# Two moves on VectorE in a two-layer attention and MLP kernel: the low halves of normalized tiles, and the reciprocals of the softmax denominators

## The chip, the cores and the metric

The kernel runs on one core of one Trainium2 chip. The metric is the device time of one execution, in microseconds (us). The engines are named as in the profile: PE (TensorE), ACT (ScalarE), DVE (VectorE), POOL (GpSimd) and SP (SyncE, which here issues all DMAs from one queue, in order). PEld is the loading of weights into PE.

## The reference

The input is 2048 rows of 512 numbers. Two layers follow, each an attention (A) and an MLP (B), with the same weights in both layers:

```
x = x + A(layernorm(x));  x = x + B(layernorm(x))      # twice
A: q = x@wq in 32 heads of 16;  k = x@wk, v = x@wv, one head for all
   p = softmax(q k^T / 4) over 2048 keys;  A = concat(p v) @ wo
B: relu(x@w1) @ w2, with w1 512x1792 and w2 1792x512
```

## The kernel before

**Precision.** Dense products run in 16 bits with each operand split into a high half and a low half, xh = fp16(x) and xl = fp16(x - xh); a product is xh·wh + xl·wh + xh·wl. So every normalized tile needs both halves before it can be used. The program has a fast path, which is what is timed, and an exact path behind a flag that is computed at the end (`self.good` collects the guards for it); `self.exact` is False in the fast path.

**Units and steps.** A unit U is four heads for 512 queries in one layer: 64 units. A unit has 16 steps, one per 128 keys. A step makes scores (PE, tile fst), exponentials (ACT, tile fp) and the product with the values (PE, into facc). Some steps are "cut": DVE splits the exponentials into two 16-bit parts (`cut`, rows fp<-fp), and PE then multiplies these with 16-bit values (`cut_values`, rows facc<-fp,fvp) instead of 32-bit ones (`values`, rows facc<-fp,fva).

**After every second unit** the sums are normalized. `unit_sums` reads the attention output (foraw) and the denominators (flsum) back from DRAM. `unit_inverse` tests the denominators against two limits (the guards, into fgood), clamps them, takes reciprocals, stores these to DRAM (frd) and reads them back spread over partitions (frinv). `unit_norm` multiplies foraw by frinv and splits the result into the halves fot.

**After every eighth unit** `follow` starts a chain for 512 rows (four tiles of 128): output projection, residual, layernorm, MLP up and down, residual, and in layer 0 the layernorm and the keys and queries of layer 1. In a chain, `ln` handles tiles in pairs: statistics and normalization for both (fbst, fbmv, fxn), then `halved` for both, then `laid`, which issues one transposing DMA per tile from fxp into the operand of the next product (fxt, fxq or fxr). A chain does this at two places, behind the output projection (`added` in `chain`) and, in layer 0, behind the last MLP product (`finish`). The last chain, alone at the end, transposes on PE instead and doesn't call `halved`. The 16 tiles of the input are normalized ahead of all that by `begin` (4) and `rows` (12); the 12 go through `halved` too, all before the first chain (`self.asked` counts the chains asked for, and is 0 until then).

**Dense products between attention steps.** Dense work is a generator that yields after each small group of products. Products run in pairs (`batch`): two PSUM tiles fmisc take a first half each, a one-element copy (fseen) on DVE marks that half as done, then the second halves follow, then DVE empties them.

**The order of the work** is fixed when the program is built. A planner (`timed`, `choose`) looks ahead over scores, value products and dense work, and picks the next item for PE by an account (`_Account`) of when each engine, tile and DMA will be free, with costs from `duration`. The account prices a subtraction of 128x512 on POOL at 0.2 + 512/530 and on DVE at 0.15 + 512/960 microseconds. `cut_some`, `early_for` and `soon` read it too: cuts are taken only when the account has DVE free, `unit_inverse` and `unit_norm` are put off to a later step while their inputs are not there, and a generator pauses until its operands are there. Every engine then executes its instructions in the order in which they were issued.

Almost all instructions have line L193, a helper's, in the profile, so tiles tell them apart.

Of the kernel before, what the change touches and what calls it, by code (L numbers as in the profile page):

```python
# [9 lines left out]
F32 = mybir.dt.float32  # L10
# [5 lines left out]
ALU = mybir.AluOpType  # L16
AX = mybir.AxisListType.X
MAX, MUL, SUB, ADD = ALU.max, ALU.mult, ALU.subtract, ALU.add
# [3 lines left out]
D = 512  # L22
# [7 lines left out]
LMIN, LMAX = 64.0, 1e30  # L30
# [194 lines left out]
class _Net:  # L225
# [319 lines left out]
    def halved(self, xn):  # L545

        xp = self.wt("xp", [P, 2, D], F16, bufs=4)
        self.nc.vector.tensor_copy(xp[:, 0], xn)
        self.nc.gpsimd.tensor_sub(xp[:, 1], xn, xp[:, 0])
        return xp  # L550

    def laid(self, xp, s, to):
# [878 lines left out]
    def unit_inverse(self, U):  # L1431
        nc = self.nc
        o, l = self.ol[U]
        if not self.exact:
            for lim, op in ((LMIN, ALU.is_ge), (LMAX, ALU.is_le)):
                nc.vector.scalar_tensor_tensor(self.good, l[:, 0], lim, self.good, op0=op, op1=MUL)
            nc.vector.tensor_scalar(l[:, 0], l[:, 0], LMIN, LMAX, op0=MAX, op1=ALU.min)
        nc.vector.reciprocal(l[:, 1], l[:, 0])
        rd = self.dp.tile([8, D], F32, name=self.tag + "rd", bufs=2)
        nc.sync.dma_start(rd.rearrange("h (c x) -> h c x", x=32), l[:, 1])  # L1440
        r = self.wt("rinv", [P, D], bufs=1 if self.exact else 2)
        nc.sync.dma_start(r, rd[:, None, :].to_broadcast([8, DH, D]))
        self.ol[U] = (o, r)
# [490 lines left out]
```

## Time and profile before

| | |
|---|---|
| median of 3 runs | 2221.99 us (2221.96 to 2226.26) |
| the profiled execution's own time | 2222.0 us |
| its span, first to last instruction | 2220.2 us |
| granted TensorE clock | 0.997 |

A row of the profile names the line, the engine, the operation, the tiles as out<-in, the shapes and the count; then total busy us and mean ns of one, or in the timeline the start and the length in us, with the idle time before it and what ended it in brackets. Rows that say x2 or x24 merge neighbouring instructions.

### The profile page before, as it was taken

Reading aid. Unit: us, or ns where it says so; the run is one execution under the profiler, and the core shown is the slowest. Engines: PE = TensorE matmul, PEld = TensorE weight load, DVE = VectorE, ACT = ScalarE, POOL = GpSimd, SP = SyncE. Lnnn points to the kernel's source line nnn. Section 1 sums busy time; section 2 is a strip of 40 time slices with the busy share of each in tenths; the row PEclk is TensorE's granted clock in tenths of the full one; section 3 lists DMA queues with packets and bytes.
Section 4 is the critical chain, followed back from the end, with each engine's and each line's share of the span. In section 5 each row is a group of like instructions: output and inputs, shape, how many; then the busy total and the mean of one; then the engine's idle time right before and its main releaser. Section 6 shows DMA issues by size and latency. Waiting matters only on the chain.

```text
span 2220.2 us, 127161 instructions
## 1 busy us (share of the span) xinstructions
PE 2151.6 (97%) x59833; PEld 1305.7 (59%) x59833; DVE 1188.3 (54%) x1931; ACT 1981.0 (89%) x2112; POOL 278.8 (13%) x318
## 2 busy tenths in 40 slices
PE   7999999999999999999999999999999999999998
PEld 3444446656667755555556755566655666675543
DVE  6526545554665565545575676555635555544442
ACT  6999999999999999999988889988999999999910
POOL 6317720001200021000120021100000000100000
PEclk9999999999999999999999999999999999999999
DMA  6336633212322143221341154431124211321222
GB/s 155 84 116 186 196 96 100 69 40 60 83 95 69 46 120 64 74 68 40 89 134 64 39 143 143 145 86 66 40 74 119 68 47 63 84 63 56 75 78 73
DMA packets 182800, 195.07 MB, mean 88 GB/s; under 512 B 79560, under 2 KB 115960, under 8 KB 182008
## 3 DMA queue, kind: packets, MB, share of 16 engines
q1 hardware_dynamic: 182264, 186.83, 28.8%
q8 instruction: 469, 7.68, 1.4%
q14 instruction: 67, 0.55, 0.1%
HBM read 120.16 MB, written 51.87 MB: 77 GB/s over the span
## 4 chain that ended last, share of the span: by engine, by line
PE 80%; ACT 11%; DVE 3%; DMA 3%; issue 2%; POOL 1%; SPq 0%; ACTq 0%; POOLq 0%; DVEq 0%
PE facc L193 31%; PE fmisc L193 28%; PE fst L193 20%; ACT fp L193 11%; DMA frd<-flsum 1%; DVE fxt L193 1%; DMA frinv<-frd 1%; DVE fbst L193 1%; SPq L193 0%; POOL fxp L193 0%; DMA fqop<-fqd 0%; DVE faccs L193 0%; POOL fbmv L193 0%; DMA fxq<-fxp 0%; DMA fqd<-fqh 0%
## 5 line engine op out<-in xcount | busy, mean ns | idle before, releaser
L193 ACT ACTIVATE fp<-fst 128x1024 f32<-128x1024 f32 x2048 | 1948.9, 1030 | 127.7 <-PE fst L193 114.7
L193 PE MATMUL fst<-fqop,fkop 64*32 64x512 f16 x16384 | 965.3, 378 | 42.6 <-ACT fp L193 32.6
L193 PE MATMUL facc<-fp,fva 64*32 64x512 f32 x13632 | 955.5, 591 | 2.0 <-DVE faccs L193 1.2
L193 PEld LDWEIGHTS <-fkop 64*32 64x32 f16 x16384 | 392.7, 91 | 457.9 <-issue 355.2
L193 DVE TENSOR_TENSOR fp<-fp 128x1024 f16<-128x1024 f32 x344 | 463.0, 1398 | 267.4 <-ACT fp L193 267.3
L193 PEld LDWEIGHTS facc<-fp,fva 64*32 64x32 f32 x13632 | 311.1, 106 | 92.3 <-issue 27.1
L193 PEld LDWEIGHTS <-fw 64*32 64x32 f16 (+1 forms) x9576 | 221.4, 93 | 108.0 <-issue 34.5
L193 PE MATMUL fmisc<-fw,fhh 64*32 64x512 f16 x6272 | 280.2, 376 | 1.1 <-DVE fseen L193 0.5
L193 POOL TENSOR_SCALAR fbmv<-fbmv 128x1 f32<-128x1 f32 x64 | 18.7, 293 | 1553.3 <-DVE fbmv L193 1552.5
L193 PE MATMUL fmisc<-fxt,fw 64*32 64x512 f16 x5376 | 199.2, 376 | 1.2 <-issue 1.0
L193 PEld LDWEIGHTS <-fhh 64*32 64x32 f16 (+1 forms) x6384 | 144.1, 93 | 78.0 <-issue 32.8
L193 PE MATMUL fmisc<-fw,fhl 64*32 64x512 f16 x3136 | 181.7, 376 | 0.0
L193 PE MATMUL facc<-fp,fvp 64*32 64x512 f16 (+2 forms) x4128 | 166.5, 387 | 0.0
L193 DVE SCALAR_TENSOR_TENSOR fxt<-fmisc,fxt 128x512 f32<-128x512 f32 x140 | 91.5, 682 | 137.1 <-PE fmisc L193 136.9
L193 PE MATMUL fmisc<-fxq,fw 64*32 64x512 f16 x4032 | 157.4, 376 | 0.3 <-DVE fhl L193 0.2
L193 DVE COPY fseen<-fmisc 1x1 f32<-1x1 f32 x266 | 29.2, 141 | 223.7 <-PE fmisc L193 219.7
L193 DVE TENSOR_TENSOR faccs<-faccs,facc 128x512 f32<-128x512 f32 x116 | 79.6, 686 | 64.2 <-PE facc L193 54.7
L193 DVE TENSOR_SCALAR fhh<-fmisc 128x512 f16<-128x512 f32 x98 | 67.0, 684 | 82.4 <-PE fmisc L193 82.3
L193 PE MATMUL fmisc<-fwo,fot 64*32 64x512 f16 x2688 | 106.3, 376 | 3.9 <-DVE fqr L193 1.9
L193 PEld LDWEIGHTS <-fvp 64*32 64x32 f16 (+1 forms) x4128 | 88.2, 90 | 33.6 <-issue 8.3
L193 PEld LDWEIGHTS <-fhl 64*32 64x32 f16 (+1 forms) x3192 | 73.6, 93 | 28.8 <-issue 4.5
L193 PEld LDWEIGHTS <-fot 64*32 64x32 f16 (+1 forms) x2736 | 59.4, 93 | 41.7 <-issue 16.5
(157 smaller groups left out, 1222.2 us busy)
## 6 DMA issues: line engine op xcount, KB each, us to landing
fw<-fwd SPq DMA_DIRECT2D x224, 256.0 KB
fod<-faccs SPq DMA_DIRECT2D x62, 256.0 KB
fqop<-fqd SPq DMA_DIRECT2D x152, 98.0 KB
fxt<-in_A_x_dram SPq DMA_DIRECT2D x32, 256.0 KB
fqd<-fqh SPq DMA_DIRECT2D x64, 128.0 KB
foraw<-fod SPq DMA_DIRECT2D x31, 256.0 KB
frinv<-frd SPq DMA_DIRECT2D x31, 256.0 KB
faccs<-in_B_w_dram SPq DMA_DIRECT2D x28, 256.0 KB
```

Source lines behind the costliest of these rows:

```text
L193: r = fn(*a, **k)
```

## The change

In `halved`, the low half is subtracted on DVE instead of POOL once a chain has been asked for; the tiles before that stay on POOL. In `unit_inverse`, the clamped denominators go into the second half of the tile, the reciprocal is taken there in place, and the store to DRAM is issued; only then come the two guards, which read the unclamped denominators. The read-back stays behind the store.

```
         xp = self.wt("xp", [P, 2, D], F16, bufs=4)
         self.nc.vector.tensor_copy(xp[:, 0], xn)
-        self.nc.gpsimd.tensor_sub(xp[:, 1], xn, xp[:, 0])
+        (self.nc.vector if self.asked else self.nc.gpsimd).tensor_sub(xp[:, 1], xn, xp[:, 0])
         return xp
...
         o, l = self.ol[U]
         if not self.exact:
+            nc.vector.tensor_scalar(l[:, 1], l[:, 0], LMIN, LMAX, op0=MAX, op1=ALU.min)
+        nc.vector.reciprocal(l[:, 1], l[:, 0 if self.exact else 1])
+        rd = self.dp.tile([8, D], F32, name=self.tag + "rd", bufs=2)
+        nc.sync.dma_start(rd.rearrange("h (c x) -> h c x", x=32), l[:, 1])
+        if not self.exact:
             for lim, op in ((LMIN, ALU.is_ge), (LMAX, ALU.is_le)):
                 nc.vector.scalar_tensor_tensor(self.good, l[:, 0], lim, self.good, op0=op, op1=MUL)
-            nc.vector.tensor_scalar(l[:, 0], l[:, 0], LMIN, LMAX, op0=MAX, op1=ALU.min)
-        nc.vector.reciprocal(l[:, 1], l[:, 0])
-        rd = self.dp.tile([8, D], F32, name=self.tag + "rd", bufs=2)
-        nc.sync.dma_start(rd.rearrange("h (c x) -> h c x", x=32), l[:, 1])
         r = self.wt("rinv", [P, D], bufs=1 if self.exact else 2)
         nc.sync.dma_start(r, rd[:, None, :].to_broadcast([8, DH, D]))
```

## The prediction

> **What bounds the kernel.** I read the page's busy times first, then the sums by stretch, then the waits of TensorE.
>
> ```profile
> span 2220.2 us, 127161 instructions
> PE 2151.6 (97%) x59833; PEld 1305.7 (59%) x59833; DVE 1188.3 (54%) x1931; ACT 1981.0 (89%) x2112; POOL 278.8 (13%) x318
> ```
>
> The first moved subtraction stands at 317 us and the last at 1919 us, so the stretch that matters is 300 to 2090 us (columns: length, then busy us of PE, PEld, DVE, ACT, POOL):
>
> ```profile
> 300.00:2090.00 1790.00, 1759.00 (x52161) 1111.76 (x52153) 976.64 (x1502) 1673.20 (x1765) 116.49 (x155) 1.00 0.28 79
> ```
>
> PE is idle for 1790.00 - 1759.00 = 31.0 us of it, 1.7%, at a granted clock of 1.00. PE sets the time. DVE has 1790.00 - 976.64 = 813 us free. Any gain has to come out of those 31 us, or out of less work on PE. What PE says it waits for there (total us, times, longest):
>
> ```profile
> PE fst L193 <- ACT fp L193: 17.5, 42, 1.2
> ...
> PE fmisc L193 <- DVE fseen L193: 0.9, 3, 0.4
> PE facc L193 <- DVE faccs L193: 0.8, 1, 0.8
> ...
> PE fmisc L193 <- DMA fxq<-fxp: 0.6, 1, 0.6
> ```
>
> More than half of the idle time is PE waiting for an exponential: moments at which the dense work (projections, MLP) has run out, so that attention goes on at ACT's pace. The tiles of the change appear with 0.6 us. So the question is how much sooner or later the change brings dense work in those moments.
>
> **The change, part by part.** The moved operation and its neighbours, from the view of the tile fxp (min/median/max ns) and from the groups by form for the same stretch (total us, mean ns):
>
> ```profile
> L193 DVE CAST fxp<-fxn x44: 417/420/423, 316.9 to 1917.8; 128x512 f16<-128x512 f32 x44
> L193 POOL TENSOR_TENSOR fxp<-fxn,fxp x44: 1148/1270/3525, 317.4 to 1919.2; 128x512 f16<-128x512 f32 x44
> ...
> L193 DVE TENSOR_TENSOR fp<-fp 128x1024 f16<-128x1024 f32 x340 | 457.6, 1398 | 263.0 <-ACT fp L193 262.9
> ...
> L193 DVE TENSOR_TENSOR fot<-foraw,fot 128x512 f16<-128x512 f32 x27 | 18.7, 692 | 0.9
> ...
> L193 DVE SCALAR_TENSOR_TENSOR fgood<-flsum,fgood 128x32 f32<-128x32 f32 x54 | 15.0, 278 | 3.7 <-DMA flsum<-fod 2.8
> ```
>
> All 44 subtractions of this stretch move. On DVE one has the shape and types of fot<-foraw,fot, so I take 0.69 us: 44 x 0.69 = 30.4 us more on DVE, 44 x 1.27 = 55.9 us less on POOL. They come in pairs (two tiles, then two transposing DMAs), 22 pairs.
>
> *Term A, transposes sooner.* Two places show a pair on its way (DVE, POOL, SP, PE rows of the timeline):
>
> ```profile
> 548.42 0.75 DVE L193 CAST fxp<-fxn 128x512 f16<-128x512 f32 x2
> 549.09 2.27 DVE L193 SCALAR_TENSOR_TENSOR fgood<-flsum,fgood 128x32 f32<-128x32 f32 x2
> ...
> 551.61 0.35 DVE L193 RECIPROCAL flsum<-flsum 128x32 f32<-128x32 f32 x1
> 548.92 2.39 POOL L193 TENSOR_TENSOR fxp<-fxn,fxp 128x512 f16<-128x512 f32 x2 [1.00 <-DVE fxp L193]
> 550.21 2.65 SPq L193 DMA_TRANSPOSE fxq<-fxp  x2
> 552.96 0.53 SPq L193 DMA_DIRECT2D frd<-flsum  x1
> ```
>
> ```profile
> 1120.00 0.76 DVE L193 CAST fxp<-fxn 128x512 f16<-128x512 f32 x2
> 1120.67 0.68 DVE L193 TENSOR_TENSOR faccs<-faccs,facc 128x512 f32<-128x512 f32 x1
> 1121.27 3.01 DVE L193 TENSOR_TENSOR fp<-fp 128x1024 f16<-128x1024 f32 x2
> 1120.50 4.77 POOL L193 TENSOR_TENSOR fxp<-fxn,fxp 128x512 f16<-128x512 f32 x2 [0.99 <-DVE fxp L193]
> 1121.81 5.39 SPq L193 DMA_TRANSPOSE fxq<-fxp  x2
> 1128.52 0.41 PE L193 MATMUL fmisc<-fxq,fwkh 64*32 64x512 f16 x8 [0.59 <-DMA fxq<-fxp]
> ```
>
> Before, the pair's last low half ends 548.92 + 2.39 - 548.42 = 2.9 us after the first cast starts. On DVE it takes 0.42 + 0.69 + 0.42 + 0.69 = 2.2 us, so it is ready 0.7 us sooner. At 1120 the cuts of the exponentials (fp<-fp) on DVE and the subtraction on POOL held each other up: 4.77 us for a pair instead of 2.39. There the pair would be ready at 1122.2 instead of 1125.3, 3.0 us sooner. Each pair's transposes land this much earlier, but PE only gains where it idles until they land. I looked at the first product that reads each transposed block. In four places it comes within about 5 us of the second transpose's issue; at the other handovers 10 us or more lie between, filled with other dense work. The four, from the first subtraction to that product:
>
> ```profile
> 333.00:340.00 7.00, 5.91 (x129) 2.41 (x129) 0.33 (x2) 7.00 (x8) 2.39 (x2) 1.00 0.79 124
> 548.92:556.78 7.86, 6.53 (x153) 2.75 (x145) 2.94 (x5) 7.86 (x10) 2.39 (x2) 1.00 0.50 113
> 1120.50:1128.52 8.02, 5.43 (x122) 2.21 (x121) 6.91 (x7) 7.94 (x10) 4.77 (x2) 1.00 0.41 73
> 1445.02:1452.34 7.32, 6.42 (x139) 2.86 (x145) 3.79 (x4) 7.32 (x9) 2.85 (x2) 1.00 0.71 117
> ```
>
> PE is idle for 16%, 17%, 32% and 12% of them; the rest is attention that must be done anyway, so a wait shortened by d gives back d times that share. The shortenings are 0.7, 0.7, 3.0 and, with a POOL pair of 2.85 instead of 2.39, 1.2 us; times the shares: 0.1 + 0.1 + 1.0 + 0.1 = 1.3 us. Bounds: nothing, where the planner puts the products at the same place in PE's order; 5.6 us, where each shortening counts whole. I take -1.3.
>
> *Term B, what now stands behind the subtractions on DVE.* DVE works in order. A pair keeps it 2 x 0.69 = 1.38 us longer. Behind 17 of the 22 pairs other work follows without a long enough pause, usually the fseen copies that let the second half of a batch of products start, or the faccs additions that free the accumulators. First and last of them:
>
> ```profile
> 540.12 0.20 DVE L193 COPY fseen<-fmisc 1x1 f32<-1x1 f32 x2
> 1918.16 0.20 DVE L193 COPY fseen<-fmisc 1x1 f32<-1x1 f32 x2
> ```
>
> At three pairs the blocked DVE gives time back. The guards at 549.09 took 2.27 us for two, against a mean of 2 x 0.28, and two more rows show it again:
>
> ```profile
> 1429.02 2.29 DVE L193 SCALAR_TENSOR_TENSOR fgood<-flsum,fgood 128x32 f32<-128x32 f32 x2
> 1445.19 1.65 DVE L193 TENSOR_TENSOR foraw<-foraw,frinv 128x512 f32<-128x512 f32 x1
> ```
>
> That is about 1.7 + 1.7 + 1.0 = 4.4 us of DVE, and these three pairs delay nothing. The other 14 pairs delay what follows by up to 1.38 us: 19.3 us. PE's waits for fseen and faccs are 1.7 us in all so far, because scores and value products fill in. With that cover, the delay costs the idle share of the whole stretch: 19.3 x 1.7% = 0.3 us. If the cover is used up as in the four windows (17%) it costs 3.3 us, and 6.2 us at the 32% of the worst one. Below zero it can't go, since nothing behind a pair comes sooner. I take +0.3, the row for the stretch, since PE's waits there are nearest to it.
>
> *Term C, reciprocals ahead of the guards.* The clamp now writes l[:, 1], the reciprocal works in place, and the store and its read-back are issued with the same neighbours on SP; no queue entry is passed. Two guards of 0.28 us no longer stand before the store: 0.56 us. At 549 that is worth nothing by itself: the reciprocal ended at 551.96, but the store waited until 552.96 behind the two transposes on SP. What waits for the read-back is the multiply of the attention output:
>
> ```profile
> DVE foraw L193 <- DMA frinv<-frd: 8.5, 4, 3.3
> ```
>
> Four waits of 27 units. Each shortens by at most 0.56 us, 2.2 us in all; at the 17% idle share of the second window 0.4 us. I take -0.4; bounds 0 and -2.2. The guards come later by the clamp and the reciprocal, and nobody waits for them before the end.
>
> *Term D, cuts.* A step whose exponentials are cut into two 16-bit halves on DVE is cheaper on PE:
>
> ```profile
> 1124.98 1.05 PE L193 MATMUL facc<-fp,fva 64*32 64x512 f32 x16
> ...
> 1128.73 0.87 PE L193 MATMUL facc<-fp,fvp 64*32 64x512 bf16 x24
> ```
>
> 0.18 us for each of the 170 cut steps (340 halves). The planner cuts only when its own account has DVE free. DVE gets 30.4 - 4.4 = 26 us more of work; at 2 x 1.40 us per cut that is at most 9 cuts lost, 1.7 us. In proportion to DVE's 813 free us it is 3%, 5 cuts, 0.9 us; a lost chance is often followed by another one step later, so I take half, +0.4. More cuts than now is possible too, because the order is made anew: -1.7 as the other bound.
>
> Sum: -1.3 + 0.3 - 0.4 + 0.4 = -1.0 us. The profiled execution took 2222.0 us, 1.8 us outside the span, and the median of the runs is 2221.99, so the forecast is 2221.0.
>
> One edge of the move shows in this pair of rows, a POOL subtraction that reads SBUF beside a DVE operation with two SBUF inputs, which takes 1.54 us here:
>
> ```profile
> 563.29 1.59 POOL L193 TENSOR_TENSOR fkop<-fkv,fkop 16x512 f16<-16x512 f32 x1 [11.99 <-DVE fkop L193]
> 563.89 1.54 DVE L193 TENSOR_TENSOR foraw<-foraw,frinv 128x512 f32<-128x512 f32 x1
> ```
>
> [...]
>
> **The rivals.** *Handovers count whole (faster).* The shortenings of term A come whole, 5.6 us, and those of C too, 2.2 us, with B and D as taken: -7.1 us, 2214.9. For it: at 1120 PE did wait for the transpose itself. Against: that is one place of 22.
>
> *The subtractions hold up the second halves of batches (slower).* The place is the fseen copies behind a pair, and it decides where a pair's batch has its second half still to come and no other dense work is open. Then the 14 pairs cost 6.2 us, the cuts 1.7, less 1.3 and 0.4: +6.2 us, 2228.2. For it: at 540 and 1918 the copies stand directly behind the casts, so DVE is already late there. Against: PE's wait for fseen is 0.9 us.
>
> *The order is made anew.* The planner accounts the subtraction on DVE and the earlier store, so from the first unit on its choices can differ everywhere, with no cause in one place. If a tenth of the 31 us of idle time and a tenth of the 170 cuts (17 x 0.18 = 3.1 us) go one way, that is 6.2 us: 2215 or 2228.
>
> *It does nothing.* The store waits behind the transposes as at 552.96, and the tiles were covered anyway: 2222.0. That lies inside the forecast's case.
>
> **How the numbers follow.** Runs of this kernel tell a change from none at about 0.2%, 4.4 us: 2217.6 to 2226.4. Forecast (with the case of nothing) 0.42, own range 2218 to 2225. Handovers whole 0.23; subtractions in the way 0.16; a new order that is better 0.11, worse 0.08. So faster 0.34, within 0.42, slower 0.24. The time is that of the likeliest, 2221.0. The range takes in both rivals' times and half as much again of the new order, 2211 to 2230.
>
> **What would show it.** Right: 12 subtractions on POOL and 44 on DVE at 0.69 us; no guard near 1.2 us beside one; a pair's casts and subtractions in 2.2 us; PE's waits for fseen and faccs under 3 us and its idle time in the stretch 27 to 34 us; 165 to 175 cuts. Wrong: PE idle 6 us more with fseen or faccs as releaser (slower rival), idle 5 us less in the windows before the transposed tiles (faster rival), or a number of cuts or idle places that moved where no pair and no unit is near (new order).

## The result and the profile after

The changed kernel takes 2238.8 us in the median (2233.96 to 2243.14) against 2221.99 us before (2219.23 to 2226.26): a ratio of 1.0075, with a 95% interval of 1.006 to 1.009. It is slower by 17 us. The forecast was 2221.0 us, a change too small to be told from none.

Single executions of one kernel scatter by some 5 us to either side. So below, a verdict on a kernel is always its ratio to the kernel before, timed on the same chip; a profile, which is one execution, is used for places and mechanisms. The profiled execution of the changed kernel took 2239.67 us. Its busy times:

```profile
span 2237.9 us, 127153 instructions
PE 2161.5 (97%) x59849; PEld 1250.8 (56%) x59849; DVE 1211.0 (54%) x1979; ACT 1981.5 (89%) x2112; POOL 223.9 (10%) x274
```

The span is 17.7 us longer. PE is busy 9.9 us longer (2161.5 against 2151.6) with 16 products more (59849 against 59833), and idle 7.8 us longer (76.4 against 68.6). Both have to be explained. POOL gave up 54.9 us and DVE took on 22.7 us, about as worked out.

The tiles of the two edits (min/median/max ns), then the cuts, from the page's groups:

```profile
L193 DVE CAST fxp<-fxn x44: 417/420/458, 315.7 to 1933.2; 128x512 f16<-128x512 f32 x44
L193 DVE TENSOR_TENSOR fxp<-fxn,fxp x44: 691/692/694, 316.1 to 1933.6; 128x512 f16<-128x512 f32 x44
L193 DVE SCALAR_TENSOR_TENSOR fgood<-flsum,fgood x54: 125/160/194, 365.4 to 2084.0; 128x32 f32<-128x32 f32 x54
```

```profile
L193 DVE TENSOR_TENSOR fp<-fp 128x1024 f16<-128x1024 f32 x348 | 467.4, 1394 | 236.2 <-ACT fp L193 235.9
```

The 44 subtractions take 0.692 us each, the guards at most 0.194 us, and 348 halves are 174 cut steps, 344 of them (172 steps) between 300 and 2105 us. The same guards before:

```profile
L193 DVE SCALAR_TENSOR_TENSOR fgood<-flsum,fgood x54: 164/192/1159, 361.8 to 2063.0; 128x32 f32<-128x32 f32 x54
```

What PE waits for between 300 and 2105 us (total us, times, longest):

```profile
PE fst L193 <- ACT fp L193: 19.1, 45, 1.0
PE facc L193 <- DVE faccs L193: 5.7, 4, 2.4
PE fmisc L193 <- issue: 5.4, 9, 1.0
PE fst L193 <- issue: 4.8, 5, 1.6
PE fmisc L193 <- DVE fseen L193: 0.8, 3, 0.3
PE facc L193 <- DVE fseen L193: 0.6, 1, 0.6
```

Before, faccs stood there with 0.8 us, once, and fseen with 0.9. The wait for a transposed block (fxq, 0.6 us) is gone; that is the gain the change was read for. In its place come 4.9 us more of waiting for accumulators, some more for exponentials (17.5 before), and 3.2 us more of "issue", idle time for which the profile shows no releaser.

A long wait and what stands ahead of it, from the timeline of the changed kernel:

```profile
315.66 0.42 DVE L193 CAST fxp<-fxn 128x512 f16<-128x512 f32 x1
316.11 0.69 DVE L193 TENSOR_TENSOR fxp<-fxn,fxp 128x512 f16<-128x512 f32 x1
316.72 0.42 DVE L193 CAST fxp<-fxn 128x512 f16<-128x512 f32 x1
317.17 0.69 DVE L193 TENSOR_TENSOR fxp<-fxn,fxp 128x512 f16<-128x512 f32 x1
317.78 0.68 DVE L193 TENSOR_TENSOR faccs<-faccs,facc 128x512 f32<-128x512 f32 x1
...
318.52 0.66 PE L193 MATMUL facc<-fp,fva 64*32 64x512 f32 x7 [2.38 <-DVE faccs L193]
```

The pair takes 317.17 + 0.69 - 315.66 = 2.2 us, as predicted. But an accumulator's last addition stands behind it, and PE's next product for that accumulator waits for it: 2.38 us. In the kernel before, the corresponding additions stand ahead of the layernorm and of the pair's casts, so nothing of the pair is in their way:

```profile
309.80 0.69 DVE L193 COPY faccs<-facc 128x512 f32<-128x512 f32 x1 [4.90 <-PE facc L193]
310.60 0.69 DVE L193 TENSOR_TENSOR faccs<-faccs,facc 128x512 f32<-128x512 f32 x1
...
312.17 0.69 DVE L193 SCALAR_TENSOR_TENSOR fxt<-fmisc,fxt 128x512 f32<-128x512 f32 x1 [0.89 <-PE fmisc L193]
...
316.95 0.76 DVE L193 CAST fxp<-fxn 128x512 f16<-128x512 f32 x2
```

So two things differ at this one place: the order, and what the order puts behind the subtractions. That is what the experiments take apart.

### The profile page after: what moved, and what is told of

The parts are those of the page before. It is cut to its first block, busy times and chain, and to the rows that moved or that the text cites. A ratio compares the mean times of both kernels' runs of the same rounds, so it can differ in the third digit from the quotient of the medians.

```text
span 2237.9 us, 127153 instructions
## 1 busy us (share of the span) xinstructions
PE 2161.5 (97%) x59849; PEld 1250.8 (56%) x59849; DVE 1211.0 (54%) x1979; ACT 1981.5 (89%) x2112; POOL 223.9 (10%) x274
## 4 chain that ended last, share of the span: by engine, by line
PE 81%; ACT 13%; DVE 3%; issue 2%; POOL 0%; DMA 0%; SPq 0%; ACTq 0%; DVEq 0%; POOLq 0%
PE facc L193 32%; PE fmisc L193 29%; PE fst L193 20%; ACT fp L193 13%; DVE fbst L193 0%; DVE fxt L193 0%; DVE fkop L193 0%; DVE faccs L193 0%; DVE fxp L193 0%; DVE fp L193 0%; POOL fbmv L193 0%; DVE fkv L193 0%; DVE fxn L193 0%; DMA fqop<-fqd 0%; SPq L193 0%
## 5 line engine op out<-in xcount | busy, mean ns | idle before, releaser
L193 PEld LDWEIGHTS <-fkop 64*32 64x32 f16 x16384 | 387.1, 91 | 483.1 <-issue 369.0
L193 PEld LDWEIGHTS facc<-fp,fva 64*32 64x32 f32 x13600 | 303.9, 106 | 106.5 <-issue 23.6
L193 PEld LDWEIGHTS <-fw 64*32 64x32 f16 (+1 forms) x9576 | 206.3, 93 | 123.0 <-issue 34.4
L193 PEld LDWEIGHTS <-fhh 64*32 64x32 f16 (+1 forms) x6384 | 135.4, 93 | 88.8 <-issue 32.6
L193 PE MATMUL facc<-fp,fvp 64*32 64x512 bf16 (+2 forms) x4176 | 166.0, 386 | 0.2 <-issue 0.2
L193 PEld LDWEIGHTS <-fvp 64*32 64x32 f16 (+1 forms) x4176 | 82.3, 90 | 40.2 <-issue 8.9
```

The costliest lines, as they stand in the source:

```text
L193: r = fn(*a, **k)
```

## The experiments

Two theories. *The hold-up*: 44 x 0.69 us more on DVE delay what stands behind them, wherever that is. *The order*: the planner's account reads the subtraction as DVE work and the store as earlier, and from there on builds another order of all engines, which happens to be slower. The kernels below differ only in which engine executes an operation, when, and in what the account is told, which can be set apart: `account` in the diffs charges an operation that is executed elsewhere.

All comparisons in one table; each interval is 95%.

| kernel | order of the work | low halves on | guards | ratio to before |
|---|---|---|---|---|
| second edit alone | new | POOL | behind | 1.0024 [1.0011, 1.0036] |
| first edit alone | new | DVE | ahead | 1.0042 [1.0029, 1.0056] |
| both, order of before | before | DVE | behind | 1.0066 [1.0049, 1.0083] |
| neither, order of after | after | POOL | ahead | 1.0057 [1.0039, 1.0075] |
| tiles 0, 1 alone | before | DVE for half | ahead | 1.0022 [1.0010, 1.0034] |
| tiles 2, 3 alone | before | DVE for half | ahead | 1.0049 [1.0034, 1.0065] |
| before, redrawn 0.21 | new | POOL | ahead | 1.0011 [0.9998, 1.0024] |
| before, redrawn 0.19 | new | POOL | ahead | 1.0020 [1.0004, 1.0035] |
| after, timed again | after | DVE | behind | 1.0090 [1.0073, 1.0106] |
| neither, both entries, 0.21 | new | POOL | ahead | 1.0076 [1.0062, 1.0091] |
| neither, both entries, 0.19 | new | POOL | ahead | 1.0064 [1.0049, 1.0080] |
| after, redrawn 0.21 | as two above | DVE | behind | 1.0109 [1.0092, 1.0126] |
| neither, entry of the first edit | as first edit alone | POOL | ahead | 1.0028 [1.0018, 1.0039] |
| the same, 0.21 | new | POOL | ahead | 1.0033 [1.0020, 1.0046] |
| second edit alone, 0.21 | new | POOL | behind | 1.0035 [1.0021, 1.0049] |
| second edit alone, 0.19 | new | POOL | behind | 1.0031 [1.0016, 1.0045] |
| second edit, order of before | before | POOL | behind | 0.9994 [0.9982, 1.0005] |
| guards ahead, order of the second edit | as second edit alone | POOL | ahead | 1.0036 [1.0022, 1.0050] |

"Redrawn" kernels have another price in the account, for every operation on POOL, so that the planner builds another order without any operation moving to another engine. A row that names an order of another row has the same instructions on PE and ACT, and the same DMAs on SP, in the same order as that row.

### Each edit alone

First the kernel with only the lines of `unit_inverse` changed, then the one with only the line of `halved`:

```
         if not self.exact:
+            nc.vector.tensor_scalar(l[:, 1], l[:, 0], LMIN, LMAX, op0=MAX, op1=ALU.min)
+        nc.vector.reciprocal(l[:, 1], l[:, 0 if self.exact else 1])
...
```

```
-        self.nc.gpsimd.tensor_sub(xp[:, 1], xn, xp[:, 0])
+        (self.nc.vector if self.asked else self.nc.gpsimd).tensor_sub(xp[:, 1], xn, xp[:, 0])
```

> Only the second edit: the reciprocals and their store ahead of the guards, the low halves stay on POOL. Theory 1 (the subtractions on DVE hold up what stands behind them, above all the faccs additions that free the accumulators): no subtraction has moved, so 2219 to 2225 us, and PE's wait for faccs stays near 0.8 us. Theory 2 (the planner's new order is worse by itself): the earlier store changes the account too, so any time between 2215 and 2240 us is possible.

> Only the first edit: the low halves on DVE, the guards ahead of the reciprocals as before. Theory 1: the whole loss is here, 2234 to 2244 us, with some 5 us of PE waiting for faccs. Theory 2: again a new order, any time between 2215 and 2245 us.

Measured 1.0024 and 1.0042. Neither edit is free, and the two sum to 0.66%, near the whole. The hold-up alone expected nothing in the first and the whole loss in the second, 2234 to 2244 us; the medians are 2222.6 and 2227.2 us, beside 2218.1 us for the kernel before on that chip. So the hold-up is not all of it; how much each way costs this doesn't yet say.

### The edits with the order held fixed

The changed operations are executed, but the account is charged as before, so that PE, ACT and SP get the work of the kernel before in the same order:

```
-        self.nc.gpsimd.tensor_sub(xp[:, 1], xn, xp[:, 0])
+        if self.asked:
+            self.tc.nc.vector.tensor_sub(xp[:, 1], xn, xp[:, 0])          # real
+            self.account("POOL", "tensor_sub", xp[:, 1], [xn, xp[:, 0]])  # charged
... # unit_inverse likewise: order of after executed, order of before charged
```

> Both edits are executed, but the planner's account is charged as if they were not: PE, ACT and SP get exactly the order of the kernel before. Theory 1 (direct hold-up on DVE): still slower than before, 2232 to 2245 us, with PE waiting for faccs or fseen at pairs. Theory 2 (the order is what costs): 2218 to 2224 us.

And the reverse: POOL subtracts and the guards stand ahead, as before, but the account is charged as after, which gives exactly the order of after:

```
-        self.nc.gpsimd.tensor_sub(xp[:, 1], xn, xp[:, 0])
+        if self.asked:
+            self.tc.nc.gpsimd.tensor_sub(xp[:, 1], xn, xp[:, 0])          # real
+            self.account("DVE", "tensor_sub", xp[:, 1], [xn, xp[:, 0]])   # charged
... # unit_inverse likewise: order of before executed, order of after charged
```

> The reverse: neither edit is executed (low halves on POOL, guards first), but the account is charged as if they were, so that PE, ACT and SP get exactly the order of the changed kernel. Theory 1: 2218 to 2226 us, since DVE no longer holds anything up. Theory 2: 2233 to 2244 us, like the changed kernel.

Measured 1.0066 and 1.0057. Each of the two alone makes more than half of the loss, and they don't add up: in the order of before the operations cost 0.66%, in the order of after only what is left to the changed kernel, 0.75 - 0.57 = 0.18% by its first comparison.

In the first of the two nothing but the moved operations differs from the kernel before. What PE waits for there, 300 to 2120 us:

```profile
PE fst L193 <- ACT fp L193: 16.8, 41, 1.2
PE fmisc L193 <- DVE fseen L193: 10.1, 10, 1.7
PE fmisc L193 <- issue: 3.1, 4, 0.9
PE facc L193 <- DVE fseen L193: 2.5, 3, 1.5
```

PE waits 10.1 + 2.5 = 12.6 us for fseen, 0.9 before. Not all of that is new idle time: between 300 and 2090 us PE is idle for 1790.00 - 1750.97 = 39.0 us against 31.0, since other waits grew shorter. One of the ten, from its timeline:

```profile
538.81 0.42 DVE L193 CAST fxp<-fxn 128x512 f16<-128x512 f32 x1
...
539.26 0.69 DVE L550 TENSOR_TENSOR fxp<-fxn,fxp 128x512 f16<-128x512 f32 x1
...
539.87 0.42 DVE L193 CAST fxp<-fxn 128x512 f16<-128x512 f32 x1
...
540.33 0.69 DVE L550 TENSOR_TENSOR fxp<-fxn,fxp 128x512 f16<-128x512 f32 x1
540.94 0.20 DVE L193 COPY fseen<-fmisc 1x1 f32<-1x1 f32 x2
541.19 0.63 PE L193 MATMUL fmisc<-fw,fhh 64*32 64x512 f16 x16 [0.83 <-DVE fseen L193]
```

Before, the same copies stood at 540.12 (the prediction quotes the row) directly behind the casts, and PE's products show no wait:

```profile
539.45 0.76 DVE L193 CAST fxp<-fxn 128x512 f16<-128x512 f32 x2
...
540.69 0.74 PE L193 MATMUL fmisc<-fw,fhh 64*32 64x512 f16 x16
```

One step of scores and values covered the copies, but not 1.38 us more.

In the second, the order of after with POOL's subtractions, the place at 316 us shows the order's own part. Its timeline:

```profile
314.50 0.76 DVE L193 CAST fxp<-fxn 128x512 f16<-128x512 f32 x2
315.17 0.68 DVE L193 TENSOR_TENSOR faccs<-faccs,facc 128x512 f32<-128x512 f32 x1
...
315.90 0.66 PE L193 MATMUL facc<-fp,fva 64*32 64x512 f32 x7 [0.93 <-DVE faccs L193]
```

PE waits 0.93 us for the late addition even without the subtractions; with both on DVE, 2 x 0.69 us later, it waits 2.38 us. At this place the order makes the collision, and the subtractions lengthen it. It is one place of 0.93 us. In the profiled execution of this kernel, the fastest of its six (2223.2 us), PE is idle for 1805.00 - 1772.85 = 32.2 us between 300 and 2105 us, 31.0 before; so this profile doesn't show where the rest of the order's 0.57% goes.

### Which pairs hold up

In the order of before, only the first pair at each of a chain's places on DVE (tiles 0 and 1), or only the second (2 and 3):

```
+    def halved(self, xn, r=None):
...
+        if r is not None and r < 2:     # or: r > 1
+            self.tc.nc.vector.tensor_sub(xp[:, 1], xn, xp[:, 0])
+            self.account("POOL", "tensor_sub", xp[:, 1], [xn, xp[:, 0]])
```

> In the order of the kernel before (the account is not told), only the first pair of each handover (tiles 0 and 1) has its low halves on DVE: 22 subtractions; guards as before. Theory 1a (what is lost is the fseen copies that stand behind first pairs and let a batch's second half start): nearly all of the direct loss, 8 to 13 us more than before, with 8 to 12 us of PE waiting for fseen. Theory 1b (any pair on DVE costs alike): half of it, 5 to 8 us.

> The same for the second pair (tiles 2 and 3), behind which the handover to the next product comes. Theory 1a: no loss or a small gain from the earlier transposes, between 5 us less and 2 us more than before. Theory 1b: 5 to 8 us more.

Measured 1.0022 and 1.0049: both cost, the second pairs more, so the expected division between them was wrong. PE's waits for fseen, first in the kernel with the first pairs, then in the one with the second:

```profile
PE fmisc L193 <- DVE fseen L193: 5.7, 7, 1.6
```

```profile
PE fmisc L193 <- DVE fseen L193: 5.4, 6, 1.7
...
PE facc L193 <- DVE fseen L193: 2.6, 3, 1.6
```

Together 13.7 us, about the 12.6 us of both at once, and 0.22 + 0.49 = 0.71% is about the 0.66%. So the hold-up looks like a sum over places. That the second pairs cost more than twice the first with 8.0 against 5.7 us of these waits is not explained.

### Is any new order slower?

The kernel before with the account's fixed price of an operation on POOL at 0.21 or 0.19 us in place of 0.2:

```
-            return 0.2 + n / 530
+            return 0.21 + n / 530      # or 0.19
```

> The kernel before with nothing changed but one price in the planner's account: an operation on POOL costs 0.21 in place of 0.20 us plus its length. The work and the engines are the same and the order on PE is another one. Theory 2a (a redrawn order is by itself slower than the one the kernel had): 4 to 12 us more than before. Theory 2b (the order of the changed kernel is worse because the account knows of the busier DVE): within 4 us of before.

> The same with a price of 0.19 us. Theory 2a: 4 to 12 us more than before. Theory 2b: within 4 us of before.

Measured 1.0011 and 1.0020. A new order alone, without any moved work, costs 0.1 to 0.2% in these two draws, the first of which can't be told from nothing: the order of before seems to be a good draw. So part of every new order's cost may be only that. The next four ask whether orders from a busier account are worse than that: the changed kernel again, the engines of before with both edits' entries in the account under both prices, and the changed kernel under the first:

```
+            self.tc.nc.gpsimd.tensor_sub(xp[:, 1], xn, xp[:, 0])          # as in neither, order of after
+            self.account("DVE", "tensor_sub", xp[:, 1], [xn, xp[:, 0]])
...
-            return 0.2 + n / 530
+            return 0.21 + n / 530      # or 0.19
```

> The changed kernel once more, on the chip of the runs it stands beside here. By the first comparison 0.6 to 0.9% slower than before. If direct hold-up and order simply added up it would be 1.2%.

> Engines of before, with an account charged as if both edits were made (as in the run with the order of after), and the account's price of a POOL operation at 0.21 in place of 0.20 us, so that the order is redrawn. Theory 3a (an account that knows of the busier DVE makes worse orders in general): 0.35 to 0.7% slower than before. Theory 3b (the order of the changed kernel was an unlucky draw): 0 to 0.25% slower, like the two redraws of the kernel before.

> The same with 0.19 us. Theory 3a: 0.35 to 0.7% slower than before. Theory 3b: 0 to 0.25%.

> The changed kernel, both edits executed and accounted, with the price at 0.21: exactly the order on PE, ACT and SP of the first redraw with a busy account, so the difference of the two is the direct effect of the edits in an order that knows of them. Direct hold-up: 0.1 to 0.4% slower than that redraw, with PE waits for faccs and fseen. No hold-up left once the planner knows: equal within 0.1%.

Measured 1.0090, 1.0076, 1.0064 and 1.0109. The three orders built with both entries but run with the engines of before (with the 1.0057 above) lie at 0.57 to 0.76%, above both plain redraws. On top of that come the executed edits. In the redrawn order, on one chip, they cost 1.09 - 0.76 = 0.33%, in the order of after 0.90 - 0.57 = 0.33% or, with the first comparison, 0.18%; each is uncertain by about 0.23% (the two half-widths, 0.16 each, combined as squares). That is 4 to 7 us of 2220.

### Which entry makes the order

Only the entry of the first edit, engines as before; then the same with the price 0.21 on POOL:

```
+            self.tc.nc.gpsimd.tensor_sub(xp[:, 1], xn, xp[:, 0])
+            self.sim.run("DVE", ..., duration("DVE", "tensor_sub", ...))
```

> Engines of before; the account is charged for the low halves on DVE alone (not for the second edit): on PE, ACT and SP exactly the order of the run with only the first edit. Theory 4a (it takes both entries in the account to make the bad orders): 0 to 0.25% slower than before. Theory 4b (the entry for the low halves is enough): 0.4 to 0.75%. Theory 4c (the entry for the earlier store is what does it): 0 to 0.25%.

> The same, redrawn with a POOL price of 0.21 us. Theory 4a: 0 to 0.25% slower than before. 4b: 0.4 to 0.75%. 4c: 0 to 0.25%.

The second edit alone under two more prices, 0.21 and then 0.19:

> Only the second edit, executed and accounted, redrawn with a POOL price of 0.21 us. Theory 4a and 4b: 0.1 to 0.3% slower than before, like the first draw of it. Theory 4c: 0.4 to 0.75%.

> The same with 0.19 us. Theory 4a and 4b: 0.1 to 0.3% slower than before. Theory 4c: 0.4 to 0.75%.

Measured 1.0028 and 1.0033 for the first entry, 1.0035 and 1.0031 for the second edit (1.0024 above). Each makes an order that is about 0.3% slower. That lies between the expectations, of which one kind was up to 0.25 or 0.3% and the other from 0.4% on. The first edit, executed in the order of its own entry, costs 0.42 - 0.28 = 0.14% on top, uncertain by 0.17%.

Last, the second edit taken apart like both were: executed in the order of before (shown), and its order with the guards executed ahead as before:

```
         if not self.exact:
+            for _ in range(2):
+                self.account("DVE", "scalar_tensor_tensor", self.good, [l[:, 0], self.good])
+            self.account("DVE", "tensor_scalar", l[:, 0], [l[:, 0]])
+            self.account("DVE", "reciprocal", l[:, 1], [l[:, 0]])
+            real.tensor_scalar(l[:, 1], l[:, 0], LMIN, LMAX, op0=MAX, op1=ALU.min)
+        real.reciprocal(l[:, 1], l[:, 0 if self.exact else 1])
... # the store, then the guards on real, not charged again
```

> Only the second edit, executed but not accounted: reciprocals ahead of the guards in exactly the order of the kernel before on PE, ACT and SP. Theory 5a (the second edit costs only through the order that its entry makes): 2214 to 2219 us, within 0.1% of before or a little faster, since only the store leaves sooner. Theory 5b (something of the edit itself costs): 4 to 9 us more than before.

> The reverse: guards first as in the kernel before, the account charged for the second edit, so that PE, ACT and SP have the order of the run with only the second edit. Theory 5a: 4 to 9 us more than before. Theory 5b: within 0.15% of before.

Measured 0.9994 [0.9982, 1.0005] and 1.0036. Executing the second edit costs nothing that can be measured; its 0.3% is the order. The first of the two has the lowest ratio of all, and it can't be told from the kernel before.

## Why the prediction was wrong, step by step

The loss of the changed kernel, 0.75% and 0.90% in its two comparisons, is made of three parts that the runs set apart, each to within some 0.2%: about 0.3% for the order from the first entry, about 0.3% for the order from the second (0.57% for both together), and 0.1 to 0.3% (3 to 7 us) for what the subtractions hold up within an order that was made for them. These are times as measured, so each holds its share of slower clock, which the last section bounds.

- **Term B failed: its price.** The prediction had the mechanism and the amount of delay, 19.3 us over 14 pairs, and priced it by the idle share of the whole stretch, 1.7%: +0.3 us. In the order of before, where nothing else differs, PE's waits for fseen grew by 12.6 - 0.9 = 11.7 us, 61% of the 19.3, and the time by 0.66% (14.6 us). That is also far above the 6.2 us that the prediction took as the most. The idle share says how often PE waits while the order suits the delays; it doesn't say how much room the order has left. The room had to be read at each place: how much PE work stands between the batch's first half and its second. At 540 it was one step.
- **The sum had no term for the order.** The prediction named a new order as a rival, at 6.2 us either way, 0.11 for better and 0.08 for worse. Measured with the engines of before, the new order costs 0.57% (12.7 us), with its redraws 0.64 and 0.76%. It was symmetric in the prediction; all of the ten other orders that were run with the subtractions on POOL lie above before, one of them with an interval that reaches 1. And it was an alternative to the other rivals. It came together with the hold-up: 6.2 + 6.2 = 12.4 us from the prediction's own two prices would have been 2234.4 us, outside its range but near the 2238.8.
- **The rival of the subtractions in the way** was priced at +6.2 us; executed in an order that was made for them they cost 3 to 7 us. Right in size there, and less than half of the 14.6 in the order of before. It had a chance of 0.16. The argument against it, that PE's wait for fseen was 0.9 us, was the error of term B again. In the changed kernel it shows as faccs, 5.7 us, more than as fseen, 1.4: in its new order it is mostly the additions that stand behind subtractions. Whether that is because the planner now knew of the subtractions is not shown; in the changed kernel redrawn with 0.21 PE's longest wait, 2.7 us, is for fseen again.
- **Term A** was right in what it removes (a pair in 2.2 us, no wait for fxq) and can't be checked in size: the wait for fxq was 0.6 us, and 1.3 us is far below what the others cost.
- **Term C** is borne out as far as it can be: -0.4 us is 0.02%, and the second edit in the order of before measured -0.06% [-0.18, +0.05], which takes in nothing too.
- **Term D** stayed inside its bounds of some 9 cuts fewer or more (1.7 us at 0.18), but the sign was the other one: 174 cuts against 172 in the whole kernel before, two more, where +0.4 us stood for two fewer.
- **The signs.** 44 subtractions at 0.692 us, no guard near 1.2 us and 165 to 175 cuts (172 in the stretch) came true. PE's waits for fseen and faccs were to stay under 3 us and its idle time under 34: they are 7.1 us and, by the row below for 300 to 2105 us, 1805.00 - 1765.95 = 39.1 us. "PE idle 6 us more with fseen or faccs as releaser" was written down as what would show the slower rival; idle is 8 us more, and 5.4 of it have these releasers.

```profile
300.00:2105.00 1805.00, 1765.95 (x52121) 1055.04 (x52113) 999.91 (x1550) 1673.00 (x1763) 60.94 (x111) 1.00 0.27 78
```

DVE operations took longer beside some POOL operations, and the change took away part of that. In the kernel before, two guards took 2.27 us at 549 us and 2.29 us at 1429 us beside subtractions on POOL, and 0.81 or 0.82 us at 813, 878 and 1360 us beside another POOL operation (fsq<-fqh); the median of one is 192 ns. With the subtractions off POOL and the guards later, the longest guard fell from 1159 to 194 ns. foraw<-foraw,frinv, 689 ns in the median, still took 1541 ns at 570 us beside fkop<-fkv,fkop, as in the prediction's rows at 563.89 us. None of the moved subtractions was held in its turn: all 44 took 691 to 694 ns. No run shows that PE gained by the freed time.

Two things stay open. Why the entries make slower orders than plain redraws is not known; one collision (0.93 us at 316 us) is all that was traced of it. And with two plain redraws against eight orders with entries, that they are worse as a class is likely and not settled: 1.0020 and 1.0024 nearly touch.

## What to carry to other kernels

An engine that is busy 54% of the time was not a free place for 30 us of work here: the work behind it waited its turn (PE's waits for fseen went from 0.9 to 12.6 us in the order of before), and the price was decided by what stood behind each moved instruction and by how much other work its reader had until then. Where a program builds its order from a cost account, an edit is two edits, the operation and the entry; run each with the other held fixed, and redraw the order by a meaningless change of price, before a cause is believed or a saving is hoped for. Rivals that can happen together are added in the forecast, not set side by side.

## What was not expected of the hardware

Of the 17.7 us of span, 9.9 are PE being busy longer at almost the same number of products. Stretches of the changed kernel, in pairs (the columns end with the granted clock, the DMA share and GB/s):

```profile
569.40:572.80 3.40, 1.96 (x34) 0.43 (x18) 3.30 (x5) 3.18 (x5) 1.59 (x1) 1.00 0.47 164
572.80:576.20 3.40, 2.83 (x41) 1.37 (x48) 2.93 (x9) 0.93 (x2) 0.00 (x0) 0.51 0.22 82
1129.20:1132.60 3.40, 1.42 (x32) 0.34 (x24) 2.58 (x7) 3.40 (x6) 1.68 (x4) 1.00 0.45 159
1132.60:1139.40 6.80, 6.07 (x73) 1.80 (x80) 5.56 (x8) 4.88 (x7) 0.00 (x0) 0.50 0.56 125
1378.40:1381.80 3.40, 1.79 (x51) 0.69 (x51) 3.26 (x6) 3.31 (x4) 1.92 (x2) 1.00 0.45 130
1381.80:1385.20 3.40, 3.40 (x42) 1.59 (x36) 2.70 (x5) 2.40 (x3) 0.00 (x0) 0.50 0.56 194
```

In each pair PE is idle for about half of 3.4 us (1.44, 1.98 and 1.61 us), and in the next 3.4 us (once 6.8) the granted clock is 0.50 or 0.51. In the two traces of before and after these drops begin on a grid of 3.41 us. In the changed kernel they begin at 572.84, 1132.62, 1381.79 and 2149.79 us, which are 164, 73 and 225 times 3.413 us apart. Each trace has one more in the start, from 29.72 us before and 30.12 us after, and one at the end, from 2217.66 and 2235.13 us; in the kernel before these two, 641 times 3.413 us apart, are the only ones. Counted from the first instruction the grid stands 0.4 us later in the changed kernel's execution. Other profiles have drops too: from 1085 to 1180 us the granted clock is 0.96 with the first edit alone, with neither edit executed under both entries (the order of after and its two redraws) and in the changed kernel timed again, 0.98 in the changed kernel redrawn with 0.21, and 1.00 in the kernel before.

Between 60 and 2135 us of the changed kernel the three drops follow cells of the grid in which PE was idle for 59%, 47% and 42% (from 1129.21, 1378.38 and 569.42 us). Three other cells, from 316.84, 1433.00 and 873.21 us, were idle for 49%, 46% and 42% and have no drop behind them. The first two of these, and the cell ahead of a fourth drop, in the tail, each with the cell that follows it:

```profile
316.84:320.25 3.41, 1.73 (x48) 1.02 (x56) 1.59 (x3) 0.31 (x1) 0.00 (x0) 1.00 0.66 127
320.25:323.66 3.41, 3.41 (x104) 2.33 (x95) 0.23 (x2) 3.20 (x4) 0.00 (x0) 1.00 0.94 155
1433.00:1436.41 3.41, 1.82 (x77) 1.12 (x79) 1.60 (x2) 1.58 (x3) 0.00 (x0) 1.00 0.56 193
1436.41:1439.82 3.41, 3.09 (x104) 1.72 (x96) 1.09 (x1) 3.17 (x4) 0.00 (x0) 1.00 0.45 146
2146.38:2149.79 3.41, 1.47 (x24) 0.58 (x22) 3.23 (x8) 1.52 (x3) 0.94 (x2) 1.00 0.00 0
2149.79:2153.20 3.41, 3.41 (x52) 2.18 (x52) 2.43 (x4) 0.62 (x2) 0.00 (x0) 0.50 0.02 5
```

The drops last 3.4 + 6.8 + 3.4 us, and the fourth 3.4: 17 us at half clock. In that fourth drop 16 products took 1.19 us, and after it 0.63 us:

```profile
2150.83 1.19 PE L193 MATMUL fmisc<-fw,fhh 64*32 64x512 f16 x16
...
2157.25 0.63 PE L193 MATMUL fmisc<-fw,fhh 64*32 64x512 f16 x16
```

So up to 17 x 0.5 = 8.5 us were lost, an estimate from these lengths and the clock of 0.5, which can be most of the 9.9. The profiled execution of the kernel before had no drop between its start and its end, though it had an idle place at 562 us, which the grid cut in two, and one cell, the last row, that was idle for longer than two of the three ahead of a drop above:

```profile
562.20:565.60 3.40, 2.05 (x45) 0.88 (x30) 3.24 (x6) 3.40 (x5) 1.59 (x1) 1.00 0.69 245
565.60:569.00 3.40, 2.57 (x56) 1.02 (x56) 2.62 (x9) 1.69 (x3) 0.00 (x0) 1.00 0.20 78
1408.70:1412.10 3.40, 1.64 (x36) 0.72 (x36) 2.61 (x5) 2.79 (x4) 0.00 (x0) 1.00 1.03 338
```

40% and 24% idle, then 52%. So the idle share of a cell doesn't decide alone, and what else does is not shown. A wait may have cost twice here, once itself and once through the clock; with cells on both sides that is an estimate. Of the whole loss this is a part: the six executions of the changed kernel timed again have a granted clock of 0.9942 in the mean, the eleven of the kernel before beside them 0.9967, so at most 0.0025 x 2237 = 5.6 us of the 18.8 between their medians went through the clock. For the two kernels that take the edits and the order apart, the same working gives at most 2.7 us (both, order of before) and 2.4 us (neither, order of after).
